# Another order for the first part of a hand-ordered attention-and-maxout kernel

## The chip, the cores and the metric

The kernel runs on one core of one Trainium2 chip. A core has five instruction streams that run side by side: TensorE (PE, matrix products; PEld are its weight loads), VectorE (DVE), ScalarE (ACT), GpSimd (POOL) and SyncE (SP), and 16 DMA engines that SP, ACT and POOL feed through queues of their own. The metric is the device time of one execution in microseconds (us). Three executions of the kernel before gave 153.05 us as their median, 152.96 to 153.08.

## The reference

The input is `x` (8 batches, 8 heads, 512 tokens, 64 wide), `state` (8 batches, 8 heads, 32 states, 64 wide) and four weight matrices. Tokens read the states, states read the tokens, and both results go through a maxout layer with three weights and an output layer:

```python
scores = (x @ state.T) / 8;  a = softmax(scores);   xread = a @ state
scores2 = (state @ x.T) / 8; a2 = softmax(scores2); sread = a2 @ x
y = concat([xread, sread], axis=2)           # 544 rows a batch and head
y = y.transpose(0, 2, 1, 3).reshape(4352, 512)
h = max(y @ w1, y @ w2, y @ w3)              # 512 -> 768
out = h @ w_out                              # 768 -> 512
```

## The kernel before

Products run in bf16 with f32 sums. The token rows are not formed as `xread` first. For each batch the kernel multiplies the states into the weights (`G = state @ w`, one row for each head and state, 3 x 768 columns) and then `a @ G`, so that the maxout layer works on 256 rows (heads times states) in place of 512. The middle dimension 768 is cut in six slices `m` of 128 columns; a slice of the maxout layer of a batch's 512 tokens is three weights by two halves of those rows, six products of 128 x 128 x 512.

Three plans, written out by hand as strings, hold the whole order of the work: `FIRST` (batches 0 and 1, and the preparation of batches 2 and 3), `EACH` (run five times, once a batch, in a steady rhythm) and `LAST`. `perform` (L543) reads a plan and calls one function for each step; each function issues its instructions, DMAs too, on the engine that the step names (`S`, `P`, `A`, `D` for SP, POOL, ACT, DVE). An engine runs its instructions strictly in the order of issue, so the place of a step in the string is its place in the queue of its engine, and nothing else decides the order. Waits between engines follow from the data and from the buffers.

The steps that the change moves, with the numbers being batch and slice, or parity `g` of the heads (even heads are g = 0, odd ones g = 1):

- `lst k` loads the states of batches 2k and 2k+1 (L153); `stc` casts them to bf16 (L216), `stt` transposes them on PE (L221), `stp` copies them into the block-diagonal tile `bd` in two halves (L227).
- `lxu 0 0` loads the even heads of batch 0 as f32 through SP (L174) and `cxu` casts them on DVE (L177). `lxg b g` loads the other halves of x through POOL with a cast on the way (L169). `xt b g` transposes one half on PE (8 instructions, L236), `xtc` copies it to `xT` (L243). `xtd b` (L248) does it for a later batch by a DMA from SP.
- `lw m0 m1 i` loads slices m0 to m1-1 of weight i through POOL (L180), `lwo` the output weight (L185), `lx` a later batch (L164).
- `sc b g` are the scores (8 PE instructions, L261), `ex` the exponentials on ACT (L268), `sum` the row sums and their reciprocals on DVE (L275, L277), `wt` the division (L283), `at b g` turns the weights a on PE (4 instructions, L294), `atc` copies them out (L297); `atd` does it by a DMA (L301).
- `sr b` is the states' reading (32 PE instructions, L326), `srs` its scaling (L339, L342).
- `g b m` is one slice of G (8 PE instructions, L362), `gc` its copy out of PSUM (L380); `gr`, `grc` are the same over wider runs of columns (L362, L402, L405).
- `l1 b m` is one slice of the maxout layer, 6 PE instructions into three banks (L415); `m0` (ACT, L430), `ma` and `mb` (DVE, L435 and L439) take the maximum. `l2 b j` is a quarter of the output layer (6 PE instructions, L446), `l2c` its copy out (L453), `so` the store (L476).
- `busy n` issues n products of zeros on PE that nothing reads (L210). `ident` builds the identity that transposes need (POOL), `pad` makes padded copies of x (POOL, L307 and L310).

PSUM is handed out from the strings `BANKS` (four single banks, one digit for each use) and `PAIRS` (two pairs of banks, for `g`, `gr` and `sc 2`). A step that gets a bank waits until the last reader of that bank has ended; when two engines read one bank's tile in halves (`stp 0 AD`), the second half waits for the first.

Where a step names two engines (`DA`), its two halves go to the two engines in that order.

Of the kernel before, what the change touches and what calls it, by code (L numbers as in the profile page):

```python
# [15 lines left out]


FIRST = """
    lxu 0 0 S; lst 0 A; lxg 1 0; zero; warm; clr 0; clr 1; clr 2; clr 3; stc 0 D; ident; busy 1;
    lst 1 S; busy 2; busy 1; busy 2; busy 1; busy 1; stt 0; busy 1; busy 2; cxu 0 0 D; stp 0 AD;  # L20
    stc 1 A; lxg 0 1; xt 0 0; lxg 1 1; lw 0 1 0; busy 1; lw 0 3 1; xtc 0 0 A; xt 1 0; xones 0; busy 2;
    busy 1; lw 0 2 2; xtc 1 0 DA; sc 0 0; xt 0 1; lw 1 2 0; busy 1; busy 1; lw 2 4 0; lw 2 4 2; sc 1 0;
    ex 0 0; ex 1 0; busy 1; xtc 0 1 A; xt 1 1; busy 1; busy 1; sum 0 0; busy 1; stt 1; lw 3 6 1; busy 1;
    sc 0 1; busy 1; ex 0 1; xtc 1 1 D; busy 1; sc 1 1; ex 1 1; busy 1; stp 1 A; lxg 2 1; wt 0 0 P;
    busy 1; xones 1; at 0 0; sum 1 0; busy 1; busy 1; sum 0 1; sr 0; busy 1; sum 1 1; g 0 0; wt 1 0 P;
    g 1 0; gc 1 0 A; wt 0 1 D; sr 1; busy 1; srs 0; lxg 2 0; at 0 1; at 1 0; wt 1 1 P; atc 0 0 D;
    at 1 1; gc 0 0 D; atc 0 1 A; lw 4 6 2; srs 1; atc 1 0 A; g 1 1; atc 1 1 D; gc 1 1 A; g 0 1;
    l1 0 0 1; g 1 2; m0 0 0; g 0 2; l1 1 0; gc 0 1 D; gc 1 2 A; l1 1 1; m0 1 0; ma 0 0; mb 0 0; ma 1 0;
    lw 4 6 0; mb 1 0; l1 0 1; g 0 3; m0 1 1; g 1 3; gc 0 2 A; l1 0 2; ma 1 1; l1 1 2; xtd 2; pad 2;
    m0 0 1; mb 1 1; ma 0 1; m0 0 2; lst 3 A; gc 0 3 DA; l1 0 3; m0 1 2; lwo; gc 1 3 A; ones; g 0 5;  # L30
    g 1 4; mb 0 1; ma 0 2; lxg 3 0; m0 0 3; mb 0 2; gc 0 5 A; lst 2 S; ma 1 2; l1 1 3; stc 3 P; m0 1 3;
    l1 0 5; mb 1 2; g 0 4; gc 1 4 A; g 1 5; ma 0 3; l1 1 4; m0 0 5; gc 0 4 A; mb 0 3; ma 1 3; m0 1 4;
    lxg 3 1; l1 0 4; sc 2 -; gc 1 5 A; xtd 3; mb 1 3; gr 2 1024 1280; m0 0 4; gr 2 1280 1792; ex 2 -;
    grc 2 1280 1792 A; l1 1 5; m0 1 5; ma 0 5; stc 2 A; mb 0 5; gr 2 512 1024; gr 2 1792 2304; sr 2;
    ma 1 4; mb 1 4; ma 0 4; mb 0 4; l2 0 3; grc 2 512 1024 A; stt 2; grc 2 1024 1280 D; gr 2 0 512;
    l2 0 0; l2 0 1; l2 0 2; grc 2 1792 2304 A; sum 2 -; l2c 0 0 A; grc 2 0 512 A; ma 1 5; wt 2 - P;
    srs 2; l2c 0 3 A; stp 2 A; mb 1 5; l2c 0 2 D; atd 2; so 0 2 4 P; stt 3; l2c 0 1 A; stp 3 DA;
    so 0 0 2 A; lx 4;
"""
EACH = """  # L40
    pad 1; gr 1 1792 2304; gr 1 0 512; grc 1 1792 2304 AD; l2 -1 0; l2 -1 1; l1 0 0; grc 1 0 512 D;
# [22 lines left out]
"""  # L64

BANKS = """
# [3 lines left out]
"""  # L70
PAIRS = """
    0110101010 1010101010 1010101010 1010101010 10
"""


# [601 lines left out]
```

## Time and profile before

| | us |
|---|---|
| median of 3 executions | 153.05 |
| the profiled execution | 152.82 |
| its span, first to last instruction | 151.0 |
| PE busy within the span | 146.6 |
| DVE, ACT, POOL busy | 115.4, 86.2, 54.6 |
| first product of the maxout layer (L415) starts | 16.40 |
| first product of the steady part (`EACH`) starts | 42.72 |

The page sums the span by engine, shows the chain of work that ended last, and groups instructions by source line. A row of the timeline has the start in us from the span's start, the duration, the engine, the line, the operation, the tiles out<-in, the shape and a count; brackets hold the idle time before it and what ended it. A merged row's duration runs to the modelled end of its last instruction, some 0.17 us after PE could issue the next one.

### The profile page before, as it was taken

Reading aid. Unit: us, or ns where it says so; the run is one execution under the profiler, and the core shown is the slowest. Engines: PE = TensorE matmul, PEld = TensorE weight load, DVE = VectorE, ACT = ScalarE, POOL = GpSimd, SP = SyncE. Lnnn points to the kernel's source line nnn. Section 1 sums busy time; section 2 is a strip of 40 time slices with the busy share of each in tenths; the row PEclk is TensorE's granted clock in tenths of the full one; section 3 lists DMA queues with packets and bytes.
Section 4 is the critical chain, followed back from the end, with each engine's and each line's share of the span. In section 5 each row is a group of like instructions: output and inputs, shape, how many; then the busy total and the mean of one; then the engine's idle time right before and its main releaser. Section 6 shows DMA issues by size and latency. Waiting matters only on the chain.

```text
span 151.0 us, 3639 instructions
## 1 busy us (share of the span) xinstructions
PE 146.6 (97%) x1434; PEld 73.6 (49%) x1434; DVE 115.4 (76%) x202; ACT 86.2 (57%) x147; POOL 54.6 (36%) x74
## 2 busy tenths in 40 slices
PE   6999999999999999999999999999999999999992
PEld 2475434344444443444354435443544445679771
DVE  6468899889139899789978997798879887675353
ACT  3567866779695665466646664666466653331220
POOL 6998418302235505550554055404341200001500
PEclk9999999999999999999999999999999999999999
DMA  4999999994658898897599848895503250300545
GB/s 108 245 196 195 198 197 198 143 206 67 125 138 256 109 87 250 103 230 120 173 111 222 154 144 124 213 139 155 205 0 78 80 215 7 133 5 17 190 168 198
DMA packets 38581, 22.30 MB, mean 148 GB/s; under 512 B 22032, under 2 KB 36368, under 8 KB 38560
## 3 DMA queue, kind: packets, MB, share of 16 engines
q0 software_dynamic: 15200, 13.44, 47.3%
q1 hardware_dynamic: 21920, 6.95, 22.8%
q10 hardware_dynamic: 1440, 1.64, 3.6%
q8 instruction: 12, 0.20, 0.5%
q14 instruction: 9, 0.07, 0.2%
HBM read 15.20 MB, written 8.91 MB: 160 GB/s over the span
## 4 chain that ended last, share of the span: by engine, by line
PE 94%; DMA 4%; DVE 1%; issue 1%; POOLq 0%
PE pw L415 47%; PE po L446 25%; PE pg L362 6%; PE po L461 4%; DMA x<-in_x_dram 4%; PE idle L210 3%; PE ps L261 2%; PE psr L326 2%; PE pxt L236 1%; PE pgh L362 1%; PE pat L294 1%; DVE held L521 0%; PE pt L221 0%; PE idle L519 0%; DVE osb L465 0%
## 5 line engine op out<-in xcount | busy, mean ns | idle before, releaser
L415 PE MATMUL pw<-aT,G 128*128 128x512 bf16 x288 | 66.6, 379 | 0.0
L430 ACT CAST t<-pw 128x512 bf16<-128x512 f32 (+1 forms) x54 | 30.4, 562 | 28.7 <-PE pw L415 27.9
L415 PEld LDWEIGHTS <-G 128*128 128x128 bf16 x288 | 27.2, 98 | 33.7 <-issue 2.4
L435 DVE TENSOR_TENSOR t<-t,pw 128x512 bf16<-128x512 bf16 (+1 forms) x54 | 35.3, 653 | 9.9 <-ACT t L430 7.6
L446 PE MATMUL po<-wout,ht 128*128 128x512 bf16 x168 | 39.8, 379 | 0.0
L439 DVE TENSOR_TENSOR ht<-t,pw 128x512 bf16<-128x512 bf16 x48 | 33.0, 687 | 4.6
L283 POOL TENSOR_TENSOR a<-e,rden 128x1024 bf16<-128x1024 bf16 (+1 forms) x9 | 14.9, 1654 | 27.4 <-DVE seen L336 15.1
L446 PEld LDWEIGHTS <-ht 128*128 128x128 bf16 x168 | 15.3, 98 | 19.2 <-issue 2.1
L476 POOL DMA_DIRECT2D out_dram<-osb x12 | 6.9, 578 | 32.6 <-ACT t L430 22.0
L402 ACT CAST G<-pg 128x1024 bf16<-128x1024 f32 (+1 forms) x19 | 16.6, 912 | 0.8 <-PE pg L362 0.8
L453 DVE COPY osb<-po 128x512 f32<-128x512 f32 x14 | 9.6, 687 | 6.8 <-PE po L446 6.8
L310 POOL COPY xp<-x 128x1024 bf16<-128x1024 bf16 x12 | 12.3, 1066 | 5.2 <-DMA x<-in_x_dram 5.2
L453 ACT COPY osb<-po 128x512 f32<-128x512 f32 x15 | 8.9, 594 | 8.8 <-PE po L446 8.8
L275 DVE TENSOR_REDUCE seen<-e 128x32 f32<-128x1024 bf16 (+1 forms) x10 | 10.0, 999 | 2.9 <-ACT e L268 2.9
L268 ACT ACTIVATE e<-ps 128x1024 bf16<-128x1024 f32 (+1 forms) x10 | 8.5, 853 | 5.9 <-PE ps L261 5.8
L210 PE MATMUL idle<-zero 128*128 128x512 bf16 x30 | 10.2, 441 | 1.3 <-DVE zero L188 1.3
L362 PE MATMUL pg<-w,bd 64*32 64x512 bf16 (+1 forms) x288 | 10.8, 362 | 0.0
L402 DVE CAST G<-pg 128x512 bf16<-128x512 f32 (+1 forms) x10 | 9.1, 948 | 1.3 <-ACT G L402 1.3
L471 POOL DMA_DIRECT2D out_dram<-osb x4 | 2.2, 541 | 19.4 <-ACT osb L465 19.4
L380 ACT CAST G<-pg 128x768 bf16<-128x768 f32 (+1 forms) x10 | 7.7, 774 | 2.1 <-PE pg L362 2.1
L415 PE MATMUL pw<-atp,w 128*128 128x256 bf16 x72 | 8.7, 272 | 0.0
L415 PEld LDWEIGHTS <-w 128*128 128x128 bf16 x72 | 6.9, 98 | 1.5
(71 smaller groups left out, 114.1 us busy)
## 6 DMA issues: line engine op xcount, KB each, us to landing
out_dram<-osb POOLq DMA_DIRECT2D x11, 512.0 KB, 3.7
x<-in_x_dram POOLq DMA_DIRECT2D x4, 512.0 KB, 7.5
x<-in_x_dram POOLq DMA_DIRECT2D x7, 256.0 KB, 9.3
w<-in_moe_w_dram POOLq DMA_DIRECT2D x5, 256.0 KB, 8.8
w<-in_moe_w_dram POOLq DMA_DIRECT2D x2, 384.0 KB, 8.7
wout<-in_moe_w_out_dram POOLq DMA_DIRECT2D x1, 768.0 KB, 9.7
out_dram<-osb SPq DMA_DIRECT2D x3, 256.0 KB, 2.3
osb<-in_x_dram SPq DMA_DIRECT2D x1, 512.0 KB, 4.1
```

The source lines that it names most:

```text
L210: nc.tensor.matmul(p, zero[:, 0:128], zero, start=True, stop=True)
L275: nc.vector.reduce_sum(out=den, in_=parity(e[b], g), axis=AX.X)
L283: times[c](out=parity(a[b], g).rearrange("p j g s n -> p j (g s) n"), in0=parity(e[b], g).rearrange("p j g s n -> p j (g s) n"), in1=rdens ...
L310: nc.gpsimd.tensor_copy(out=xp[b][:, :, :, g * (D + 1):g * (D + 1) + D], in_=v[:, g])
L362: nc.tensor.matmul(p(s, g), bd(b, 2 * s + g)[64 * g:64 * g + 64, g, :], f(w_sb[64 * g:64 * g + 64, s]), start=True, stop=True, tile_positi ...
L402: copier[c[g]](out=v[:, g:h], in_=p[:, g:h, 0:c1 - c0])
L415: nc.tensor.matmul(pw[i][:, 0:n], lhs(i, k), rhs(k), start=(k == 0), stop=(k == nk - 1))
L430: nc.scalar.copy(out=t0s[b, m][:, 0:n], in_=open_ps["l", b, m][0][:, 0:n])
L435: nc.vector.tensor_max(t1s[b, m][:, 0:n], t0s.pop((b, m))[:, 0:n], open_ps["l", b, m][1][:, 0:n])
L439: nc.vector.tensor_max(ht[b][:, m, :], t1s.pop((b, m))[:, 0:n], open_ps.pop(("l", b, m))[2][:, 0:n])
L446: nc.tensor.matmul(p, ht[b][:, m, j * 128:(j + 1) * 128], wout_sb[:, m, :], start=(m == 0), stop=(m == NM - 1))
L453: copier[c[i]](out=o[:, j, i * w:i * w + w], in_=p[:, i * w:i * w + w])
```

## The change

Only `FIRST` is rewritten, and with it the strings of banks. The set of steps is the same but for these:

- `lw 2 4 2` (slices 2 and 3 of the third weight, one DMA) becomes `lw 2 3 2` and `lw 3 4 2`; the first now goes ahead of `lw 1 2 0`, the second behind `lxg 2 1`.
- 32 products of zeros stand in the place of 30.
- `ident` is issued behind four loads on POOL, where it was behind one. `lst 1` is on ACT, behind `stc 0`, where it was on SP right behind `lxu 0 0`.
- `stt 1` and its copies come after `sc 1 1`; `stt 2` and `stt 3` stay at the end, with `stp 2` and `stp 3` last.
- `at 1 1` (the odd weights of batch 1) comes after the first `l1`, where it was ahead of it.
- Copies change engines: among others `stc 0` DVE to ACT, `stc 1` ACT to POOL, `wt 0 0` and `wt 2` POOL to DVE, `gc 0 0` DVE to ACT, `gc 0 2` ACT to DVE; `so 0 0 2` ACT to POOL; `stc 2` ACT to DVE, both halves of `stp 3` to DVE; `gc 1 0`, `gc 0 1` and three `grc 2` are shared by ACT and DVE; `lx 4` goes ahead of both stores; `atd 2` goes ahead of `xtd 3`; `ones` is issued earlier.
- The first `l1 0 0` loses its last argument: it takes the two halves of the rows weight by weight, where it took each half for all three weights. In the tail the quarters of `l2 0` come as 3, 2, 0, 1, where they came as 3, 0, 1, 2.

`EACH` and `LAST` are unchanged as text. Their digits in `BANKS` are renamed one for one (3 to 1, 2 to 3, 1 to 2, 0 to 0) and those of `PAIRS` are swapped, so that each step there shares its banks with the same steps as before.

```diff
@@ -16,26 +16,26 @@
 
 
 FIRST = """
-    lxu 0 0 S; lst 0 A; lxg 1 0; zero; warm; clr 0; clr 1; clr 2; clr 3; stc 0 D; ident; busy 1;
-    lst 1 S; busy 2; busy 1; busy 2; busy 1; busy 1; stt 0; busy 1; busy 2; cxu 0 0 D; stp 0 AD;
-    stc 1 A; lxg 0 1; xt 0 0; lxg 1 1; lw 0 1 0; busy 1; lw 0 3 1; xtc 0 0 A; xt 1 0; xones 0; busy 2;
-    busy 1; lw 0 2 2; xtc 1 0 DA; sc 0 0; xt 0 1; lw 1 2 0; busy 1; busy 1; lw 2 4 0; lw 2 4 2; sc 1 0;
-    ex 0 0; ex 1 0; busy 1; xtc 0 1 A; xt 1 1; busy 1; busy 1; sum 0 0; busy 1; stt 1; lw 3 6 1; busy 1;
-    sc 0 1; busy 1; ex 0 1; xtc 1 1 D; busy 1; sc 1 1; ex 1 1; busy 1; stp 1 A; lxg 2 1; wt 0 0 P;
-    busy 1; xones 1; at 0 0; sum 1 0; busy 1; busy 1; sum 0 1; sr 0; busy 1; sum 1 1; g 0 0; wt 1 0 P;
-    g 1 0; gc 1 0 A; wt 0 1 D; sr 1; busy 1; srs 0; lxg 2 0; at 0 1; at 1 0; wt 1 1 P; atc 0 0 D;
-    at 1 1; gc 0 0 D; atc 0 1 A; lw 4 6 2; srs 1; atc 1 0 A; g 1 1; atc 1 1 D; gc 1 1 A; g 0 1;
-    l1 0 0 1; g 1 2; m0 0 0; g 0 2; l1 1 0; gc 0 1 D; gc 1 2 A; l1 1 1; m0 1 0; ma 0 0; mb 0 0; ma 1 0;
-    lw 4 6 0; mb 1 0; l1 0 1; g 0 3; m0 1 1; g 1 3; gc 0 2 A; l1 0 2; ma 1 1; l1 1 2; xtd 2; pad 2;
-    m0 0 1; mb 1 1; ma 0 1; m0 0 2; lst 3 A; gc 0 3 DA; l1 0 3; m0 1 2; lwo; gc 1 3 A; ones; g 0 5;
-    g 1 4; mb 0 1; ma 0 2; lxg 3 0; m0 0 3; mb 0 2; gc 0 5 A; lst 2 S; ma 1 2; l1 1 3; stc 3 P; m0 1 3;
-    l1 0 5; mb 1 2; g 0 4; gc 1 4 A; g 1 5; ma 0 3; l1 1 4; m0 0 5; gc 0 4 A; mb 0 3; ma 1 3; m0 1 4;
-    lxg 3 1; l1 0 4; sc 2 -; gc 1 5 A; xtd 3; mb 1 3; gr 2 1024 1280; m0 0 4; gr 2 1280 1792; ex 2 -;
-    grc 2 1280 1792 A; l1 1 5; m0 1 5; ma 0 5; stc 2 A; mb 0 5; gr 2 512 1024; gr 2 1792 2304; sr 2;
-    ma 1 4; mb 1 4; ma 0 4; mb 0 4; l2 0 3; grc 2 512 1024 A; stt 2; grc 2 1024 1280 D; gr 2 0 512;
-    l2 0 0; l2 0 1; l2 0 2; grc 2 1792 2304 A; sum 2 -; l2c 0 0 A; grc 2 0 512 A; ma 1 5; wt 2 - P;
-    srs 2; l2c 0 3 A; stp 2 A; mb 1 5; l2c 0 2 D; atd 2; so 0 2 4 P; stt 3; l2c 0 1 A; stp 3 DA;
-    so 0 0 2 A; lx 4;
+    lst 0 A; lxu 0 0 S; zero; clr 0; clr 1; clr 2; clr 3; warm; lxg 1 0; lxg 0 1; busy 3; busy 1;
+    lxg 1 1; busy 1; busy 1; lw 0 1 0; stc 0 A; busy 1; cxu 0 0 D; ident; busy 1; busy 1; lst 1 A;
+    busy 1; busy 1; stt 0; ones; xt 0 0; busy 1; busy 1; busy 1; xtc 0 0 D; busy 1; busy 1; lw 0 3 1;
+    stp 0 DA; busy 1; xt 1 0; xt 0 1; xtc 1 0 D; busy 1; busy 1; sc 0 0; xtc 0 1 D; xones 0; xt 1 1;
+    lw 0 2 2; sc 1 0; busy 1; ex 0 0; busy 1; xtc 1 1 A; sum 0 0; busy 1; sc 0 1; busy 1; wt 0 0 D;
+    ex 0 1; sum 0 1; lw 2 3 2; lw 1 2 0; busy 1; busy 2; ex 1 0; busy 1; busy 1; lw 2 4 0; sum 1 0;
+    sc 1 1; lw 3 6 1; stc 1 P; stt 1; busy 1; at 0 0; busy 1; busy 1; xones 1; lxg 2 1; sr 0; ex 1 1;
+    g 0 0; lw 3 4 2; wt 0 1 D; wt 1 0 P; sum 1 1; lxg 2 0; g 1 0; stp 1 A; atc 0 0 A; gc 0 0 A; sr 1;
+    at 1 0; xtd 2; wt 1 1 P; gc 1 0 DA; srs 0; at 0 1; atc 0 1 D; g 0 1; atc 1 0 D; gc 0 1 AD; srs 1;
+    lst 2 S; g 1 1; l1 0 0; m0 0 0; lw 4 6 0; lw 4 6 2; at 1 1; pad 2; gc 1 1 A; ma 0 0; mb 0 0; busy 1;
+    g 1 2; g 0 2; gc 0 2 D; atc 1 1 A; l1 1 0; m0 1 0; l1 1 1; lwo; gc 1 2 A; m0 1 1; l1 0 1; ma 1 0;
+    m0 0 1; g 1 3; mb 1 0; gc 1 3 A; g 0 3; l1 0 2; l1 1 2; ma 1 1; mb 1 1; ma 0 1; m0 0 2; gc 0 3 DA;
+    l1 0 3; lst 3 A; m0 1 2; g 0 5; m0 0 3; gc 0 5 A; g 1 4; l1 1 3; mb 0 1; l1 0 5; ma 0 2; m0 1 3;
+    mb 0 2; lxg 3 0; gc 1 4 A; stc 3 P; ma 1 2; lxg 3 1; ma 0 3; g 0 4; m0 0 5; mb 0 3; g 1 5; gc 0 4 A;
+    l1 1 4; l1 0 4; sc 2 -; mb 1 2; m0 1 4; ma 1 3; gc 1 5 A; mb 1 3; gr 2 1024 1280; gr 2 1280 1792;
+    ma 0 5; m0 0 4; ex 2 -; mb 0 5; l1 1 5; gr 2 1792 2304; ma 1 4; grc 2 1280 1792 A; gr 2 512 1024;
+    m0 1 5; mb 1 4; sr 2; ma 0 4; grc 2 1024 1280 D; mb 0 4; sum 2 -; ma 1 5; wt 2 - D; l2 0 3; srs 2;
+    l2 0 2; l2c 0 3 A; mb 1 5; stc 2 D; grc 2 512 1024 AD; l2 0 0; grc 2 1792 2304 AD; l2c 0 2 A; lx 4;
+    atd 2; stt 2; gr 2 0 512; l2 0 1; grc 2 0 512 DA; stt 3; l2c 0 0 A; xtd 3; stp 3 D; l2c 0 1 D;
+    so 0 0 2 P; so 0 2 4 P; stp 2 A;
 """
...
 BANKS = """
-    0123012301 3023123031 0131310212 1010202320 1203120312 0132103210 2312031201 3201302130 2132021320
-    1302132103 2130231032 1032103210 3102310321 3023102310 2310230213 0231032130 2130213021 3210321302
-    3103210321 0321031023 1032130231 0231032103 2130230230 2310230123 0130230120 3123023123 123013200
+    0123012301 2303032032 1201323230 3023102030 3120210332 0132103120 1321031031 2013201302 1023101320
+    1302103213 2013210312 0132013201 3201203120 1321031203 1203120310 3210312013 2103210321 0321320132
+    1031201320 1320132012 0312013210 3120312013 2013210310 3103120310 2310210310 2301231031 2312310213
+    00
 """
 PAIRS = """
-    0110101010 1010101010 1010101010 1010101010 10
+    0101011010 1010100101 0101010101 0101010101 01
 """
```

## Prediction

> **What bounds the kernel now.** I read the page first, its sum by engine and the chain.
>
> ```profile
> span 151.0 us, 3639 instructions
> ...
> PE 146.6 (97%) x1434; PEld 73.6 (49%) x1434; DVE 115.4 (76%) x202; ACT 86.2 (57%) x147; POOL 54.6 (36%) x74
> ...
> PE 94%; DMA 4%; DVE 1%; issue 1%; POOLq 0%
> ```
>
> PE is busy for 97% of the span and 94% of the chain is PE. Then I read a table by stretches: 16.40 to 33.00 and four rounds of `EACH`, of which the first round and the sum are shown.
>
> ```profile
> 46.04:61.29 15.25, 15.25 (x149) 6.82 (x148) 13.62 (x21) 8.99 (x15) 6.47 (x9) 1.00 0.85 161
> ...
> sum 77.58, PE 77.58 PEld 33.91 DVE 66.98 ACT 48.83 POOL 30.22; mean PE 15.52 PEld 6.78 DVE 13.40 ACT 9.77 POOL 6.04
> ```
>
> The columns are the stretch, its length, PE busy, PEld, DVE, ACT, POOL, the granted clock, DMA. The round is 15.25 us and PE fills it all at clock 1.00, as it fills all five stretches (77.58 of 77.58). `EACH` and `LAST` keep their text, and their banks are only renamed. So the end moves by as much as PE's position at the start of `EACH` moves, unless copies of the first part are still in the way there. The question is then PE's timeline in the head, given here for PE alone.
>
> ```profile
> 1.27 3.43 PE L210 MATMUL idle<-zero 128*128 128x512 bf16 x8 [1.27 <-DVE zero L188]
> 4.54 0.39 PE L221 MATMUL pt<-ident,st 128*128 128x128 bf16 x4
> 4.76 0.81 PE L210 MATMUL idle<-zero 128*128 128x512 bf16 x3
> 5.72 0.62 PE L236 MATMUL pxt<-ident,x 128*128 128x128 bf16 x8
> 6.17 0.38 PE L210 MATMUL idle<-zero 128*128 128x512 bf16 x1
> 6.74 0.62 PE L236 MATMUL pxt<-ident,x 128*128 128x128 bf16 x8 [0.18 <-DMA x<-in_x_dram]
> 7.19 0.81 PE L210 MATMUL idle<-zero 128*128 128x512 bf16 x3
> 7.84 0.40 PE L261 MATMUL ps<-bd,xT 128*128 128x64 bf16 x8
> 8.07 0.61 PE L236 MATMUL pxt<-ident,x 128*128 128x128 bf16 x8
> ...
> 9.44 0.62 PE L236 MATMUL pxt<-ident,x 128*128 128x128 bf16 x8
> ...
> 13.07 0.63 PE L326 MATMUL psr<-x,e 128*32 128x128 bf16 x32
> 13.63 0.39 PE L210 MATMUL idle<-zero 128*128 128x512 bf16 x1
> 13.95 0.52 PE L362 MATMUL pg<-w,bd 64*32 64x384 bf16 x16
> 14.40 0.63 PE L326 MATMUL psr<-x,e 128*32 128x128 bf16 x32
> ...
> 15.19 0.83 PE L294 MATMUL pat<-ident,a 128*128 128x128 bf16 x12
> 15.95 0.52 PE L362 MATMUL pg<-w,bd 64*32 64x384 bf16 x16
> 16.40 1.47 PE L415 MATMUL pw<-aT,G 128*128 128x512 bf16 x6
> 17.80 0.52 PE L362 MATMUL pg<-w,bd 64*32 64x384 bf16 x16
> ```
>
> Prices come from one start to the next: a product of zeros (a filler below) is 0.427 for each of the first eight (4.54 less 1.27, with a faster last one) and (7.84 - 7.19) / 3 = 0.215 later; `xt` 6.17 - 5.72 = 0.45; `sc` 8.07 - 7.84 = 0.23; `stt` and `at` 4.76 - 4.54 = 0.22; `sr` 0.56; two `g` 14.40 - 13.95 = 0.45; an entry into `sr` or `g` costs 0.10 (13.95 - 13.63 - 0.215); `l1` 17.80 - 16.40 - 0.10 = 1.30. PE's waits in the head are what these leave: 5.72 - 4.76 - 0.65 = 0.31 for the cast of x, 6.74 - 6.17 - 0.215 = 0.35 for the x of batch 1, and nothing of note later.
>
> **The change part by part.** *Up to 5.72.* Both orders have eleven fillers and `stt 0` ahead of `xt 0 0`, so PE comes to it at 5.41 either way and waits for the same cast. The loads on POOL, and how long single issues took to land:
>
> ```profile
> 2.81 1.55 POOL L169 DMA_DIRECT2D x<-in_x_dram  x2
> 6.04 3.71 POOL L180 DMA_DIRECT2D w<-in_moe_w_dram  x5
> x<-in_x_dram POOLq DMA_DIRECT2D x1, 256.0 KB, 5.2
> x<-in_x_dram POOLq DMA_DIRECT2D x1, 256.0 KB, 5.8
> w<-in_moe_w_dram POOLq DMA_DIRECT2D x1, 256.0 KB, 7.4
> stf<-in_state_dram SPq DMA_DIRECT2D x1, 128.0 KB, 7.0
> ```
>
> `ident` was over when the two loads behind it began at 2.81. It moves behind three more issues of 1.55 / 2 = 0.78 on POOL, so it is over at 5.15, `stt 0` goes at 5.2 and is done at 5.4. It costs nothing; without the wait for the cast each 0.1 that it is later would cost 0.1.
>
> *The x loads.* The x loads issued at 2.81 and 3.59 land 5.2 and 5.8 later, at 8.01 and 9.4, `lw 0 2 2` (issued at 6.04) at 13.4. In the new order the same bytes lie ahead of each of these on POOL's queue. `lst 1` (128 KB) leaves SP's queue and comes from ACT's at about 4 (an estimate: behind the cast that `stt 0` at 4.54 followed), which is still ahead of or beside those x loads, so I leave their landings where they are.
>
> *5.72 to 13.7, step by step.* `xt 0 0` to 6.17; six fillers to 7.46; `xt 1 0` to 7.91 (its x landed just before 6.74, that wait of 0.35 is gone); `xt 0 1` waits for 8.01, goes at 8.05 (0.14 of wait), to 8.50; two fillers, `sc 0 0` to 9.15; `xt 1 1` waits until 9.44 (0.29, where a filler stood before), to 9.89; `sc 1 0`, three fillers, `sc 0 1`, six fillers to 12.27; `sc 1 1`, `stt 1`, a filler, `at 0 0` to 13.15; two fillers and the entry: `sr 0` at 13.68, against 13.07. The same work is done as before 13.07; three more fillers up to here make 0.65 of the 0.61, and the new waits, 0.43, stand for old ones of 0.35 and 0.03.
>
> *13.7 to the maxout layer.* `sr 0` and an entry to 14.34 (the filler behind each `sr` is gone), two `g` to 14.79, `sr 1` to 15.35, two `at` and an entry to 15.89, two `g` to 16.34: `l1 0 0` at 16.34, against 16.40. Here PE is only a little behind ACT, whose rows are these:
>
> ```profile
> 12.58 1.16 ACT L227 COPY bd<-pt 64x512 bf16<-64x512 bf16 x2
> 14.54 0.80 ACT L380 CAST G<-pg 128x768 bf16<-128x768 f32 x1 [0.80 <-PE pg L362]
> 15.61 1.07 ACT L297 COPY aT<-pat 128x512 bf16<-128x512 bf16 x2 [0.27 <-PE pat L294]
> 17.48 0.59 ACT L430 CAST t<-pw 128x512 bf16<-128x512 f32 x1
> 14.02 1.29 POOL L283 TENSOR_TENSOR a<-e,rden 128x512 bf16<-128x512 bf16 x1 [0.40 <-DVE rden L277]
> ```
>
> `ex 1 1` starts at 12.7 (`sc 1 1` plus 0.2), then two state copies 1.16, `atc 0 0` 0.58, `gc 0 0` 0.80 end at 15.7 or a little later, and the third pair of `g` needs that at 15.89. `wt 1 0` on POOL starts at about 13.8 and takes up to 1.29; `at 1 0` needs it at 15.35. Both fit, by 0.2 and 0.3.
>
> *The turn put behind `l1 0 0`.* `l1 0 0` to 17.64, `at 1 1` 0.22, a filler 0.22, an entry, two `g`: `l1 1 0` at 18.63. Before, it came 0.45 after 17.80, at 18.25. That is +0.37 with the same work done: 0.43 for two fillers over all, 0.14 + 0.29 of new waits for the 0.35 and 0.03 that went, less 0.10 for fewer entries. The cover here is thin: `m0 0 0` starts at 16.97, and with `gc 1 1` (0.80) and `atc 1 1` (0.58) behind it ACT is done between 18.7 and 18.95, as far as starts overlap, while the second product of `l1 1 0` wants it at 18.84. Ends: 0 and 0.3 (when the whole tile must be there at 18.63 and nothing overlaps); I take 0.05.
>
> *The price of a filler.* The row at 1.27 shows eight at 0.427, the row at 4.76 three at half that. The Trainium skill, TensorE: Matmul & The Clock Gate, part 1, says that the halved clock of the start lasts for a span of time of about 3.4 us and not for a number of products. The trace agrees, with 3.3 us from the first product to the first group at the full rate. By that rule the two added fillers run at the full rate and cost 0.43 as above; at the halved clock they would cost 0.85.
>
> *From `l1 1 0` to `EACH`.* The order of `g` and `l1` on PE is the old one up to the tail, and DVE's maxima keep their distance: `gc 0 2`, the copy of a slice (ACT's take 0.80), is new on DVE, but `m0 0 0` is done at 16.97 + 0.59 = 17.56, where it was at 18.07, and `l1 1 0` comes 0.37 later, so that DVE has 0.9 more ahead of `ma 1 0`. Two old waits lie here:
>
> ```profile
> 19.63 2.75 PE L415 MATMUL pw<-aT,G 128*128 128x512 bf16 x12
> 34.04 1.63 PE L415 MATMUL pw<-aT,G 128*128 128x512 bf16 x6
> 34.68 1.01 ACT L402 CAST G<-pg 128x1024 bf16<-128x1024 f32 x1
> ```
>
> `l1 1 1` could go 1.30 after 18.25 and started at 19.63, 0.08 late, for `mb 0 0`; DVE has no room to give that back, so I count half. The group at 34.04 takes 1.63 in place of 1.47: a bank that `mb 0 4` had not read. The new banks give it others, and 0.16 goes; next late is the pair for `gr 2 512 1024`, which comes free with the copy that ends at 34.68 + 1.01 = 35.69 and would be wanted at 34.04 + 1.30 + 0.10 + 0.22 = 35.66. With the way to PE, 0.05, that leaves -0.08.
>
> *The tail.* DVE takes on `wt 2`, `stc 2`, three half copies of G and half of `stp 3`, about 4.4 us, into this gap:
>
> ```profile
> 42.60 0.69 DVE L453 COPY osb<-po 128x512 f32<-128x512 f32 x1 [4.29 <-PE po L446]
> 45.14 1.82 DVE L402 CAST G<-pg 128x512 bf16<-128x512 f32 x2 [1.25 <-ACT G L402]
> 43.27 2.76 PE L446 MATMUL po<-wout,ht 128*128 128x512 bf16 x12
> ```
>
> The gaps of 4.29 and 1.25 hold it. The closest place is the first `l2` of `EACH`: its bank waits for `l2c 0 0` on ACT, behind both halves of the last copy of G. From the end of `gr 2 0 512` that is 0.2 to DVE, 0.69 there, 0.5 from start to start on ACT (1.07 less 0.58, the row at 15.61), 0.58 and 0.05, 2.0 us in all. PE has an `l2` of 1.30, `stt 3` 0.22, an entry 0.10 and two `gr` of 0.45 or more to do, 2.1. It fits by 0.1; I count nothing. `so 0 0 2` from ACT to POOL, `lx 4` issued earlier and `atd 2` ahead of `xtd 3` touch queues on which PE waits first at `l1 2 0`, two `l2` behind the row at 43.27, 2.6 us: 0, with 0.3 as the upper end.
>
> *Sum.* +0.37 + 0.05 - 0.04 - 0.08 = +0.30 us, rounded down to +0.25 since the switch costs are the least sure. The profiled execution would go from 152.82 (span 151.0 and 1.8 around it) to 153.1; the median of the runs stands 0.23 above it, so 153.05 becomes 153.3. A measurement of this kernel can tell about 0.2%, 0.31 us, from no change, and the forecast lies inside that, on the slow side.
>
> **The rivals.** *The walk holds* (0.46): 153.3, itself between 153.1 and 153.5.
>
> *The tail is late, slower* (0.25). DVE has some nine pieces between `sum 2` and the last copy of G. If they follow each other by their full length of 0.69 and not by some 0.60, DVE is 0.8 late, the pair for `gr 2 0 512` comes free after PE asks for it, and the first `l2` of `EACH` waits. It decides from 0.1 us of lateness on; each further 0.1 costs 0.1. Price 0.3 to 0.6: about 153.7. For it speaks that DVE is the engine with the least room (13.62 of 15.25 in the round quoted), against it that its wait of 4.29 ended only with PE.
>
> *The x lands earlier, not slower* (0.18). The last row of the loads shows a state load of 128 KB beside running loads of POOL: 7.0 us to land. If `lst 1` on ACT's queue is pushed aside like that, its 128 KB of f32 are out of the x loads' way, 0.35 us, as a quarter of the 512 KB that such a load reads in the 1.4 between 8.01 and 9.4, both new waits shrink by up to 0.29, and the time is 153.0. The Trainium skill, DMA: Bandwidth & Descriptors, Queues, rings and completion order, says that a DMA engine alternates between its queues packet by packet. By that rule `lst 1` would be through within a microsecond, the x loads land as before and the time is 153.3. The 7.0 speaks against an even alternation there; which of the two holds at 4 us no row shows.
>
> *POOL is held* (0.05). `stc 1` now waits on POOL for `lst 1`, and `lxg 2 1`, `lw 3 4 2`, `wt 1 0` are queued behind it, 2.4 us of work ahead of 14.0. It decides when `lst 1` lands after 11.6, that is, 7.6 us after its issue; a microsecond beyond costs PE one at `at 1 0`: 154.3.
>
> *Otherwise* (0.06). Faster than 152.8 it cannot be by this stream: with every wait of the head gone but the cast's, it is 0.43 - 0.38 - 0.10 - 0.15 = -0.2.
>
> **How the numbers follow.** Forecast 153.3. Of the walk's 0.46, 0.32 lie within 0.2% and 0.14 above; of the tail's 0.25, 0.22 above; of the early x's 0.18, 0.15 within and 0.03 below; POOL 0.05 above; the rest in thirds. Faster 0.05, same 0.52, slower 0.43. The range takes the early x and the tail's full price: 152.9 to 153.8.
>
> **What would show it.** In PE's timeline: `xt 0 0` at 5.7 again, `xt 1 0` at 7.5 with no wait, short waits before 8.05 and 9.44; `sr 0` at 13.7, `l1 0 0` at 16.3 to 16.5, `l1 1 0` at 18.6 to 18.8, the first `l2` of `EACH` at 43.5 (43.27 before); rounds of 15.25 again. Wrong it would be by x landing well before 8.0 and 9.4, by a wait of PE for ACT or DVE ahead of the third pair of `g` or of `l1 1 0`, or by waits between 40 and 47.

## The result, and the profile after

The changed kernel took 154.21 us (median, 153.58 to 154.44) where the kernel before, measured beside it, took 153.06 (152.96 to 153.61): a ratio of 1.0061, 95% interval 1.0034 to 1.0087. By the ratio that is slower by 0.9 us (0.5 to 1.3; the two medians are 1.15 apart), where 0.25 had been forecast, and 154.21 lies above the range, which ended at 153.8. The profiled execution took 154.17 with a span of 152.4, so its trace stands for the median.

The page of the changed kernel, its sum by engine and the chain that ended last; then, from the chain in order of time, its one long piece that is not PE, and below it the one of the kernel before:

```profile
span 152.4 us, 3642 instructions
...
PE 147.3 (97%) x1436; PEld 74.2 (49%) x1436; DVE 120.7 (79%) x210; ACT 82.7 (54%) x144; POOL 53.5 (35%) x75
...
PE 91%; DMA 5%; POOL 1%; issue 1%; DVE 1%; POOLq 0%
```
```profile
3.02 7.32 DMA x<-in_x_dram
```
```profile
1.37 5.32 DMA x<-in_x_dram
```

PE is as busy as before. But its share of the chain fell from 94% to 91%: the x load that the chain goes through now lands at 10.34, where the one before landed at 6.69. The stretches from the first `l2` of `EACH` on (columns as in the prediction's table) say that the steady part is as before:

```profile
44.55:59.85 15.30, 15.30 (x156) 6.86 (x149) 13.64 (x22) 9.94 (x18) 5.49 (x7) 1.00 0.63 130
59.85:75.10 15.25, 15.25 (x156) 6.81 (x149) 12.89 (x20) 9.06 (x16) 6.02 (x8) 1.00 0.80 158
```

So the loss lies ahead of 44.55, against 43.27 before: 1.28 us in these two executions. PE's timeline of the changed kernel shows where (every line number is one higher than before; in most kernels of the experiments below it is two higher):

```profile
1.28 4.54 PE L211 MATMUL idle<-zero 128*128 128x512 bf16 x11 [1.28 <-DVE zero L189]
5.65 0.39 PE L222 MATMUL pt<-ident,st 128*128 128x128 bf16 x4
5.87 0.61 PE L237 MATMUL pxt<-ident,x 128*128 128x128 bf16 x8
6.32 1.46 PE L211 MATMUL idle<-zero 128*128 128x512 bf16 x6
7.62 0.61 PE L237 MATMUL pxt<-ident,x 128*128 128x128 bf16 x8
8.74 0.62 PE L237 MATMUL pxt<-ident,x 128*128 128x128 bf16 x8 [0.51 <-DMA x<-in_x_dram]
...
10.39 0.62 PE L237 MATMUL pxt<-ident,x 128*128 128x128 bf16 x8 [0.36 <-DMA x<-in_x_dram]
...
16.80 0.64 PE L363 MATMUL pg<-w,bd 64*32 64x384 bf16 x16
17.38 1.47 PE L416 MATMUL pw<-aT,G 128*128 128x512 bf16 x6
...
19.22 0.52 PE L363 MATMUL pg<-w,bd 64*32 64x384 bf16 x16
19.67 0.61 PE L416 MATMUL pw<-aT,G 128*128 128x512 bf16 x2
```

`xt 1 1` starts at 10.39 (9.44 before): 0.95 later. `l1 1 0` starts at 19.67 (18.25 before): 1.42 later. From the one to the other are 9.28, against 8.81. I call this the stretch below. The 1.42 is then 0.95 of x and 0.47 of stretch, and 0.14 of it is won back before 44.55.

The issues of the second and third x load and of `lst 1`, each with its time to land, and the DMA queues between 7 and 8 us (packets, MB, and the share of the 16 engines; q0 is POOL's queue, q10 ACT's), first of the changed kernel, then of the kernel before:

```profile
x<-in_x_dram POOLq DMA_DIRECT2D x1, 256.0 KB, 6.4
...
x<-in_x_dram POOLq DMA_DIRECT2D x1, 256.0 KB, 7.3
stf<-in_state_dram ACTq DMA_DIRECT2D x1, 128.0 KB, 6.2
...
q0 software_dynamic: 319, 0.16, 118.4%
q10 hardware_dynamic: 46, 0.05, 17.0%
```
```profile
q0 software_dynamic: 394, 0.19, 145.0%
```

The x loads were issued at 2.27 and 3.02, earlier than before, and landed at 8.69 and 10.35, later than the 8.01 and 9.40 of before. `lst 1`, issued on ACT at 3.67, has no packet until 7.3 and lands at 9.9, so it moves just when PE waits for x.

### The profile page after: what moved, and what is told of

Its sections match the earlier page's. It is cut to its first block, busy times and chain, and to the rows that moved or that the text cites. A ratio compares the mean times of both kernels' runs of the same rounds, so it can differ in the third digit from the quotient of the medians.

```text
span 152.4 us, 3642 instructions
## 1 busy us (share of the span) xinstructions
PE 147.3 (97%) x1436; PEld 74.2 (49%) x1436; DVE 120.7 (79%) x210; ACT 82.7 (54%) x144; POOL 53.5 (35%) x75
## 4 chain that ended last, share of the span: by engine, by line
PE 91%; DMA 5%; POOL 1%; issue 1%; DVE 1%; POOLq 0%
PE pw L416 47%; PE po L447 25%; PE pg L363 6%; DMA x<-in_x_dram 5%; PE po L462 4%; PE ps L262 2%; PE psr L327 2%; PE idle L211 2%; PE pgh L363 1%; POOL x L170 1%; PE pat L295 1%; DVE held L522 0%; PE pt L222 0%; PE pxt L237 0%; PE idle L520 0%
## 5 line engine op out<-in xcount | busy, mean ns | idle before, releaser
L477 POOL DMA_DIRECT2D out_dram<-osb x13 | 7.4, 569 | 43.9 <-ACT t L431 27.7
L284 POOL TENSOR_TENSOR a<-e,rden 128x1024 bf16<-128x1024 bf16 (+1 forms) x7 | 11.9, 1697 | 20.3 <-DVE seen L337 10.3
L403 ACT CAST G<-pg 128x1024 bf16<-128x1024 f32 (+1 forms) x19 | 15.3, 840 | 3.0 <-DVE G L403 1.9
L403 DVE CAST G<-pg 128x512 bf16<-128x512 f32 (+1 forms) x13 | 11.1, 888 | 0.1
L472 POOL DMA_DIRECT2D out_dram<-osb x4 | 2.2, 541 | 19.4 <-ACT osb L466 19.4
L181 POOL DMA_DIRECT2D w<-in_moe_w_dram x10 | 7.7, 788 | 0.0
```

Source lines behind the costliest of these rows:

```text
L284: times[c](out=parity(a[b], g).rearrange("p j g s n -> p j (g s) n"), in0=parity(e[b], g).rearrange("p j g s n -> p j (g s) n"), in1=rdens ...
L403: copier[c[g]](out=v[:, g:h], in_=p[:, g:h, 0:c1 - c0])
```

## The experiments

Three theories stood at first. **S**: the state load on ACT's queue moves among the x loads and makes them late. **P**: the x loads are late because POOL issues three in a row and `ident` behind them. **C**: the other 0.47 is the stretch, that is, fillers, scores and copies between `xt 1 1` and `l1 1 0`. In the table the x column is the landing of the last x load that `xt 1 1` needs; x, `xt 1 1`, `l1 1 0` and the stretch are of one profiled execution of each, and landings differ by some tenths from one execution to the next. The time is the median, the ratio is to the kernel before, measured beside it.

| kernel | x | `xt 1 1` | `l1 1 0` | stretch | time | ratio, 95% interval |
|---|---|---|---|---|---|---|
| before | 9.40 | 9.44 | 18.25 | 8.81 | 153.06 | |
| after | 10.35 | 10.39 | 19.67 | 9.28 | 154.21 | 1.0061, 1.0034 to 1.0087 |
| after, states on SP | 9.68 | 9.72 | 19.00 | 9.28 | 153.66 | 1.0042, 1.0024 to 1.0061 |
| before, states on ACT | 10.00 | 10.04 | 18.85 | 8.81 | 153.45 | 1.0032, 1.0013 to 1.0050 |
| after, `ident` early | 10.01 | 10.05 | 19.33 | 9.28 | 153.87 | 1.0047, 1.0031 to 1.0062 |
| after, two fillers less | 10.06 | 10.11 | 19.35 | 9.24 | 154.09 | 1.0066, 1.0044 to 1.0087 |
| after, states on POOL | 10.55 | 10.59 | 19.87 | 9.28 | 153.94 | 1.0051, 1.0034 to 1.0068 |
| the same, `ident` early | 9.66 | 9.71 | 18.99 | 9.28 | 153.71 | 1.0031, 1.0015 to 1.0047 |
| before, states on POOL | 9.41 | 9.53 | 18.92 | 9.39 | 153.55 | 1.0037, 1.0024 to 1.0050 |
| before, states behind W | 9.63 | 9.92 | 18.96 | 9.04 | 153.72 | 1.0029, 1.0015 to 1.0043 |
| before, other states early | 10.32 | 10.37 | 19.18 | 8.81 | 153.36 | 1.0008, 0.9998 to 1.0018 |
| before, other states midway | 10.21 | 10.27 | 19.09 | 8.82 | 153.48 | 1.0012, 0.9994 to 1.0031 |
| before, two fillers more | 9.73 | 9.78 | 19.02 | 9.24 | 153.64 | 1.0033, 1.0021 to 1.0045 |
| states on SP, scores early | 9.43 | 9.69 | 19.18 | 9.49 | 153.82 | 1.0046, 1.0031 to 1.0061 |
| the same, two fillers less | 9.65 | 9.71 | 19.08 | 9.37 | 153.87 | 1.0053, 1.0033 to 1.0073 |
| the same, `wt 0 1` on POOL | 9.57 | 9.61 | 18.65 | 9.04 | 153.40 | 1.0016, 1.0000 to 1.0032 |

**The states on SP again, in the new order.**

```diff
-    lst 0 A; lxu 0 0 S; zero; ... busy 1; lst 1 A;
+    lst 0 A; lxu 0 0 S; lst 1 S; zero; ... busy 1;
```

> The changed kernel with one step put back: lst 1 on SP right behind lxu 0 0, as before the change. Theory S (the state load on ACT's queue runs through the x loads): the x loads that PE waits for land at about 8.0 and 9.4 again instead of 8.7 and 10.35, PE starts xt 1 1 near 9.45 instead of 10.39, and the time falls by 0.6 to 1.0 us, to about 0.2 to 0.4 us over the kernel before. Theory P (the loads are late because they are issued on POOL without ident between them, during DVE's clearing): the x loads still land at 8.6 or later and 10.2 or later, and the time stays about 1 us over the kernel before.

The last x load landed 0.67 earlier than in the changed kernel, not quite at the 9.4 that S had promised, and the median fell by 0.55, a little less than its 0.6 to 1.0; the two intervals overlap. The stretch stayed at 9.28.

**The states on ACT, in the old order.**

```diff
-    stc 0 D; ident; busy 1; lst 1 S; ... stp 0 AD; stc 1 A; ... stt 1; lw 3 6 1;
+    stc 0 A; lst 1 A; ident; busy 1; ... stp 0 AD; ... stc 1 P; stt 1; lw 3 6 1;
```

> The kernel before with the state load alone moved: stc 0 on ACT, lst 1 on ACT behind it, and stc 1 on POOL ahead of lw 3 6 1 (so that ACT does not stand still for it). Theory S: lst 1 lands near 9.9, the second and third x loads land at about 8.7 and 10.3 instead of 8.0 and 9.4, and the kernel is 0.5 to 1.0 us slower than before. Theory P: the x loads land at 8.0 and 9.4 within 0.2, and the time is within 0.3 us of before.

The same step made the old order slower, and PE's timeline of that kernel shows x as the cause and nothing else:

```profile
8.70 0.62 PE L238 MATMUL pxt<-ident,x 128*128 128x128 bf16 x8 [0.20 <-DMA x<-in_x_dram]
10.04 0.62 PE L238 MATMUL pxt<-ident,x 128*128 128x128 bf16 x8
...
18.85 1.47 PE L417 MATMUL pw<-aT,G 128*128 128x512 bf16 x6
```

`xt 1 1` is 0.60 later than in before and `l1 1 0` is 0.60 later: the old stretch of 8.81, only moved. The median is 0.36 above the 153.09 measured beside it (0.49 by the ratio), where S had said 0.5 to 1.0.

**`ident` early, in the new order.**

```diff
-    lxg 1 0; lxg 0 1; ... cxu 0 0 D; ident; busy 1;
+    lxg 1 0; ident; lxg 0 1; ... cxu 0 0 D; busy 1;
```

> The changed kernel with ident put back behind the first x load on POOL. Theory S: nothing but ident moves, the x loads still land near 8.7 and 10.35, the time is within 0.3 us of the changed kernel (about 1 us over the kernel before). Theory P: the x loads land at 8.0 and 9.4, the time falls by 0.6 to 1.0 us.

The last x load landed at 10.01, still 0.6 late, and the time did not return. P does not explain the changed kernel.

**Two fillers less, in the new order.**

```diff
-    lw 1 2 0; busy 1; busy 2; ex 1 0; busy 1; busy 1; lw 2 4 0;
+    lw 1 2 0; busy 2; ex 1 0; busy 1; lw 2 4 0;
```

> The changed kernel with two of the six products of zeros between sc 0 1 and sc 1 1 left out. By the prediction's sum a filler is 0.215 us on PE's path: 0.43 us less. Rival: the division of batch 1's weights (POOL at 14.76 to 16.05, wanted by at 1 0 at 16.25) and the copies on ACT (gc 0 0 ends at 16.66, wanted at 16.80) take over after 0.1 to 0.2: no more than 0.2 us less.

Two products of 0.215 were taken out and the stretch fell by 0.04, from 9.28 to 9.24. The time did not move. The time came back as waits: 0.2 before one of the remaining fillers, whose cause the trace does not tell plainly, and the rest in small pieces from `at 1 0` on. `at 1 0` waits for POOL, which divides until 15.76, after waiting for DVE's reciprocals, and `g 1 1` behind it waits for ACT's half of `gc 1 0`:

```profile
14.47 1.29 POOL L285 TENSOR_TENSOR a<-e,rden 128x512 bf16<-128x512 bf16 x1 [2.45 <-DVE rden L279]
```

So C in the form "the fillers are what makes it long" falls for the new order. Whether a filler costs anything in the old order was still open.

**Two fillers more, in the old order.**

```diff
-    sc 0 1; busy 1; ex 0 1;
+    sc 0 1; busy 3; ex 0 1;
```

> The kernel before with two more fillers (0.43 of TensorE) between batch 0's odd scores and batch 1's. Theory C in the prediction's form (TensorE's own walk sets this stretch in before, so a filler is paid in full): the stretch from the last turn of x (9.44) to layer 1 of batch 1 goes from 8.81 to about 9.24 and the time to 153.4 to 153.5. Rival (the copies on ACT and DVE set it in before too, and the fillers fall into waits that stand behind them): a stretch of 9.0 or less and a time of 153.0 to 153.2.

PE's timeline of this kernel, `xt 1 1` and `l1 1 0`:

```profile
9.78 0.62 PE L238 MATMUL pxt<-ident,x 128*128 128x128 bf16 x8 [0.23 <-DMA x<-in_x_dram]
...
19.02 1.25 PE L417 MATMUL pw<-aT,G 128*128 128x512 bf16 x5
```

19.02 - 9.78 = 9.24, which is 8.81 and 0.43: in the old order PE sets the stretch and two fillers are paid in full, as the prediction priced them; the median, 153.64, is 0.52 above the 153.12 beside it. In the new order other engines have come up to the same length, so that taking the fillers away uncovers them. The next three kernels say which. All have the states on SP.

**Scores early.** Batch 1's even scores go back ahead of `xt 1 1`, into PE's wait for x, with their exponential and sum.

```diff
-    xones 0; xt 1 1; lw 0 2 2; sc 1 0; busy 1; ex 0 0; ... wt 0 0 D; ... busy 2; ex 1 0; ... sum 1 0; sc 1 1;
+    xones 0; sc 1 0; xt 1 1; lw 0 2 2; busy 1; ex 0 0; ex 1 0; ... wt 0 0 D; sum 1 0; ... busy 2; ... sc 1 1;
```

> The changed kernel with the states back on SP (153.66 in its run) and batch 1's even scores back ahead of the last turn of x, their exponential right behind batch 0's, their sum two places earlier on DVE. Theory C (the stretch from the last turn of x to layer 1 is 0.47 longer because the scores of 0.23 and one more filler of 0.22 now stand in it): the scores fill the wait of 0.29 for the last x load, the stretch falls from 9.28 to about 9.05, and the time is 153.4 to 153.5. Rival (the stretch is set by the copies and the division of batch 1's weights, not by what TensorE has in it): it stays at 9.2 or more, the time at 153.6 to 153.7.

The stretch grew to 9.49. Its timeline names what came late:

```profile
11.70 1.24 PE L212 MATMUL idle<-zero 128*128 128x512 bf16 x4 [0.30 <-ACT xT L245]
```

`xtc 1 1` on ACT now stands behind a second exponential, and a filler waited for the bank that it empties. PE's 0.23 fewer were no gain, since PE was not what set the length.

**The same with two fillers less.** Those at `busy 1` (bank 0) and the last of the six go.

```diff
-    busy 1; busy 2; busy 1; busy 1; lw 2 4 0; sc 1 1;
+    busy 2; busy 1; lw 2 4 0; sc 1 1;
```

> The kernel of the run with the early scores, and two of the six fillers between the odd scores of batch 0 and those of batch 1 left out (0.43 of TensorE's time). Theory C with the division as what held the run with two fillers less: batch 1's even weights are now divided more than a microsecond earlier, so the 0.43 is gained nearly whole, the stretch falls to about 8.65 and the time to 153.0 to 153.1. Rival (the copies on ACT between the odd scores and the second product that builds G hold it, or the copy of the last turned x): half of it or less, a stretch of 8.85 or more and a time of 153.25 or more, with waits where the fillers stood or before those products.

9.37, the rival's figure. PE's fourth product pair `g 1 1` (the second half of the group) waits, and DVE's timeline shows why; first PE, then DVE:

```profile
15.67 0.36 PE L364 MATMUL pg<-w,bd 64*32 64x384 bf16 x8
16.50 0.36 PE L364 MATMUL pg<-w,bd 64*32 64x384 bf16 x8 [0.48 <-ACT G L382]
```
```profile
11.93 0.68 DVE L277 TENSOR_REDUCE seen<-e 128x16 f32<-128x512 bf16 x1
12.64 0.25 DVE L279 RECIPROCAL rden<-seen 128x16 f32<-128x16 f32 x1
12.81 0.63 DVE L277 TENSOR_REDUCE seen<-e 128x16 f32<-128x512 bf16 x1
...
13.76 0.88 DVE L285 TENSOR_TENSOR a<-e,rden 128x512 bf16<-128x512 bf16 x1
14.57 0.67 DVE L277 TENSOR_REDUCE seen<-e 128x16 f32<-128x512 bf16 x1
15.28 0.25 DVE L279 RECIPROCAL rden<-seen 128x16 f32<-128x16 f32 x1
15.45 0.50 DVE L382 CAST G<-pg 128x384 bf16<-128x384 f32 x1
```

The wait is put down to ACT's half of `gc 1 0`, but that half follows DVE's, which begins only at 15.45. DVE had no pause from 11.93 on: sum, sum, division, sum, then the copy.

**The same with one division on POOL.**

```diff
-    lw 3 4 2; wt 0 1 D; wt 1 0 P; sum 1 1;
+    lw 3 4 2; wt 1 0 P; wt 0 1 P; sum 1 1;
```

> The kernel with the early scores and two fillers less (153.87), and the division of batch 0's odd weights moved from DVE to POOL, where it fits behind that of batch 1's even ones. Theory C, now with DVE as what holds the stretch (sum, sum, division, sum, then the half copy that frees the banks of the fourth product that builds G, which waited 0.48 at 16.50): that wait goes to 0.1 or less, the stretch from the last turn of x to layer 1 of batch 1 falls from 9.37 to about 8.9, and the time to 153.4. Rival (ACT holds it, DVE is only the last to be named): the wait stays at 0.3 or more, the stretch at 9.2 or more, the time at 153.7 to 153.9.

The wait of 0.48 is gone, DVE now waits for PE, and the time is the forecast 153.40 (0.47 less; the intervals do not overlap, if barely). DVE, then PE:

```profile
14.61 0.56 DVE L382 CAST G<-pg 128x384 bf16<-128x384 f32 x1 [0.27 <-PE pg L364]
```
```profile
15.58 0.64 PE L364 MATMUL pg<-w,bd 64*32 64x384 bf16 x16
...
17.99 0.73 PE L364 MATMUL pg<-w,bd 64*32 64x384 bf16 x16
18.65 1.68 PE L417 MATMUL pw<-aT,G 128*128 128x512 bf16 x7
```

9.04 in place of the forecast 8.9: the group at 17.99 takes 0.73 where 0.52 is usual, so 0.2 of wait stands there that I had not seen. Against the kernel with the states on SP alone, 153.66 and 9.28, these steps together are worth 0.24 of stretch and 0.26 of time, and those two intervals overlap. C holds in this form: in the new order PE's walk and DVE's chain to `gc 1 0` are about equally long, so that shortening PE's part alone paid 0.04 or nothing. A shorter DVE chain with all of PE's work left in place was not run; as the prediction's walk without waits is 9.19, it could give 0.09 at most, by estimate.

**Which part of S.** In the changed kernel POOL's stream also starts earlier, at 4.16 in place of 4.54, as SP's queue is shorter. Rival **B**: it is this start, beside the end of SP's x load, that slows the stream, not the states. Four kernels take the states out of the way by POOL's own queue:

```diff
 after:            -  lst 1 A;                 +  lxg 1 1; lst 1 P;
 after, ident:     -  cxu 0 0 D; ident;        +  lxg 1 0; ident;      (and the line above)
 before:           -  lst 1 S; ... stc 1 A;    +  lxg 1 1; lst 1 P; ... stc 1 P; stt 1;
 before, behind W: -  lst 1 S; ... stc 1 A; ... stt 1;   +  lw 0 1 0; lst 1 P; ... xtc 0 1 A; stc 1 A; ... ex 1 1; stt 1;
```

> The changed kernel with the second load of states taken from ACT's queue and put on POOL's, behind the last of the three x loads, where it cannot run beside or ahead of any of them. Theory S (the load of the states runs in the middle of the x loads and costs them 0.6 to 0.95 us): the last x load lands at 9.0 to 9.2 us, earlier than the 9.40 of before, since SP's queue no longer carries those 131 KB either; the last turn of x starts at about 9.2 (the walk, no longer the load, sets it), the first product of layer 1 for batch 1 comes 9.28 later, at 18.5, and the time is 153.1 to 153.3. Rival (the x loads are late because POOL's queue itself runs slower in this order, whatever else is moved): the last x load lands at 9.7 or later and the time is 153.7 or more.

> The run with the states on POOL's queue (153.94, last x load at 10.55) with the identity matrix made behind the first x load, as in before. Theory P (three x loads issued in a row, the identity only behind W's first slice, slow POOL's stream): the last x load lands at 9.5 or earlier, as in before with the states on POOL (9.41), and the time is 153.3 to 153.5. Rival B (the stream that starts at 4.15 beside SP's load is slowed whatever stands between the issues): it lands at 9.9 or later again, the time is 153.7 to 154.0.

> The kernel before with the second load of states on POOL's queue behind the last x load and its cast on POOL ahead of the second turn of states. Theory S: the x loads land about 0.35 earlier than in before (POOL's first packets come at about 4.2 instead of 4.54 and meet no other load), the two waits for x of 0.14 and 0.29 on TensorE go, the first product of layer 1 for batch 1 moves from 18.25 to about 17.9, and the time is 152.7 to 152.9, faster than before. Rival (W's first slices, 0.35 later behind the states, or the cast on POOL, take the gain back): 153.0 to 153.3, with a wait for W before the first product that builds G.

> The kernel before with the second load of states on POOL's queue behind the first slice of W, its cast on ACT behind the copy of batch 0's odd turned x, its turn on TensorE behind batch 1's odd scores. Theory S: nothing else moves while the x loads do; they land at about 6.4, 7.7 and 9.0, the two waits for x of 0.14 and 0.29 go, and the time is 152.75 to 152.95. Rival B (a stream of POOL that starts beside the end of SP's x load, at 4.2 instead of 4.5, is slowed and gains nothing): the last x load lands at 9.3 or later and the time is 153.0 to 153.4.

None gave what S had promised; the first, with 10.55 and 153.94, came out as its rival had it. All four streams started at 4.03 to 4.20, and the last x load landed at 9.41, 9.63, 9.66 and 10.55, with 9.40 in before: the earlier start, by 0.34 or more, bought nothing. In part these kernels made waits of their own. With `stc 1` on POOL, behind a landing at 9.74, the division that follows is late (stretch 9.39), and with the cast on ACT and `stt 1` behind `sc 1 1` the old order's stretch grew to 9.04, so their times don't measure x alone. For the 10.55 P would be an answer, though it did not explain the changed kernel, as `ident` is the only difference to the 9.66. But the 10.55 comes from the slowest of that kernel's five executions, 154.56, and the medians, 153.94 and 153.71, have overlapping intervals. What made it late stays open.

Two more kernels leave `lst 1` on SP, so that POOL starts late, and move another load of 128 KB, `lst 3`, from 23.41 to the front of ACT's queue:

```diff
 early:   -  l1 0 3; m0 1 2; lst 3 A; ...     +  clr 3; lst 3 A; stc 0 D;
 midway:  -  stc 0 D; ... lst 3 A; ...        +  clr 3; stc 0 A; lst 3 A;
```

> The kernel before with one line moved: the load of the fourth pair of states, 131 KB from ACT's queue, is issued behind the warm-up of ACT at about 3 us instead of at 23.41. The second pair stays on SP, so POOL's stream starts at 4.5 as in before. Theory S (a state load from ACT's queue that moves while the x loads do takes its bytes and some rate from them): the last x load lands at 9.8 to 10.1 instead of 9.40, and the time is 153.4 to 153.6. Rival B (what makes the x loads late is that POOL's stream starts at 4.15, beside the end of SP's x load): it starts at 4.5 here, the last x load lands at 9.3 to 9.6, and the time is 153.0 to 153.2.

> As the run before it (which issued the extra load at 1.36, so that it was through by 6 us and ahead of most of the x loads), but with the first state cast on ACT and the load of the fourth pair of states behind it, as the changed kernel has the second pair: issued at about 3.5, it moves between 6 and 9. The second pair stays on SP, so POOL's stream starts at 4.5. Theory S (it is the place in the middle of the x loads that costs): the last x load lands at 9.8 to 10.1, the time is 153.4 to 153.6. Rival B (the early start of POOL's stream is what costs): it lands at 9.3 to 9.6, the time is 153.1 to 153.3.

The first issued its load at 1.36, before the x loads moved, and so tells nothing of S and B: POOL's stream started at 4.89 and x was late with it in the profiled execution, which at 153.88 was the slowest of that kernel; its median, 153.36, is not distinguishable from before. The second is the test. The load was issued at 3.67, as in the changed kernel, and POOL's stream started at 4.46. POOL's and ACT's queues between 7 and 8 us, and `xt 1 1`:

```profile
q0 software_dynamic: 254, 0.12, 91.4%
q10 hardware_dynamic: 139, 0.13, 40.9%
```
```profile
10.27 0.61 PE L237 MATMUL pxt<-ident,x 128*128 128x128 bf16 x8
```

POOL's queue moved 0.12 MB in that microsecond where it moved 0.19 in before, and the last x load landed 0.81 later. B is not needed for the delay; the states alone do it.

How large is it? Single executions differ too much to read it from two of them. In the six kernels of the table with the second pair of states on SP and nothing added early on ACT, the last x load landed at 9.40 to 9.73; in the five with a state load from ACT's queue amid the x loads it landed at 10.00 to 10.35. The two groups do not overlap, and their middles, 9.61 and 10.06, are 0.45 apart. The 9.40 of before and the 10.35 of after, from which the 0.95 was read, are the two ends. In the median the step is worth +0.24 us here (the interval reaches from -0.06% to +0.31%, so the time alone does not show it), 0.36 with the states on ACT in the old order (0.49 by the ratio) and 0.55 in the new one (0.3 by the ratios).

No kernel tried beats the kernel before. The best, with the states on SP, the scores early, two fillers less and one division on POOL, takes back 0.8 of the 1.15 us between the medians.

## Why the prediction was wrong

**The step that failed: "The x loads".** It said that `lst 1` "is still ahead of or beside those x loads, so I leave their landings where they are". Beside them is not where they are: between 7 and 8 us `lst 1` moved 0.05 MB and POOL's queue gave way from 0.19 to 0.16 (between 7 and 9: 0.12 MB, and from 0.38 to 0.29), and the loads landed 0.68 and 0.95 later. The term was put at nothing; in the two traces it is 0.95 of the 1.04 by which `l1 1 0` missed its forecast of 18.63, and over the kernels of the table about 0.45. The other half of the 0.95 belongs to these two executions; its cause is open. The row of 7.0 us for a state load stood in the prediction, and it was read as a load pushed out of the way; it was a load that would come late and then take its share.

**The walk** was right. From `xt 1 1` to `l1 1 0` it made 18.63 - 9.44 = 9.19; the trace has 9.28. So 0.38 of the 0.47 by which the stretch grew was in the forecast. The 0.09 lies at the third pair of `g`, 0.64 long at 16.80 where 0.52 is usual. The two fits that were checked held: `gc 0 0` ended at 16.66 for the 16.80, and POOL's division at 16.05 for `at 1 0` at 16.25. What had not been timed is `gc 1 0`: DVE's half came first, ACT's ended at 17.04, and `g 1 1`, the second half of the pair, went at 17.09 where it could have gone at 17.03. `l1 0 0` then lost about as much again, waiting for DVE's copy of turned weights. DVE's half of `gc 1 0`, then ACT's `gc 0 0` and its half of `gc 1 0`:

```profile
15.94 0.50 DVE L381 CAST G<-pg 128x384 bf16<-128x384 f32 x1
15.85 1.19 ACT L381 CAST G<-pg 128x768 bf16<-128x768 f32 x2
```

The price of "0.43 for two fillers over all" was confirmed to the hundredth in the old order; that in the new order they cover a DVE chain of the same length was not seen.

**Up to 5.72**: `xt 0 0` went at 5.87, behind `stt 0` at 5.65 in place of 5.2. From the first filler to `stt 0` were 4.37, not 3.27 + 0.65, since ten of the eleven fillers went at about the slow price and not eight. It mattered little: the cast of x ended only at 5.79, and the waits for x behind it swallowed the rest.

**The turn behind `l1 0 0`**: taken at 0.05, it cost nothing; the two `g` at 19.22 end in time and `l1 1 0` follows at 0.45.

**The two old waits** were counted at -0.04 and -0.08. The shift fell from 1.42 at `l1 1 0` to 1.28 at the first `l2` of `EACH`, so -0.14: 0.07 and 0.16 of them went, and waits of about 0.07 are new in between.

**The tail** was right at nothing: from the first `l2 0` to the first `l2` of `EACH` are 44.55 - 37.81 = 6.74, before 43.27 - 36.54 = 6.73. That rival falls.

**The rivals.** "The x lands earlier" named the right load with the wrong sign. "POOL is held" did not happen: `stc 1` ran at 9.95, right when the states landed, and POOL then stood idle for 2.63 until DVE's reciprocals. A rival in which `lst 1` delays x was missing, and so the range ended too low: 153.3 and 0.45 are 153.75, just within it, and with the 0.95 of the profiled execution 154.25. That this is near the 154.21 is in part luck, as the executions of the changed kernel went from 153.58 to 154.44.

The page quoted there, the Trainium skill, DMA: Bandwidth & Descriptors, Queues, rings and completion order, has the DMA engines alternate between queues. The run with the other states midway agrees once the load moves, 0.13 MB against 0.12 in the same microsecond; in the changed kernel both queues moved too, but less evenly, 0.05 against 0.16. My reading of it, that the load would be through within a microsecond of its issue and x would land as before, did not follow: in both kernels it began more than 3 us after its issue, and what it then moved POOL's queue moved less.

## What to carry to other kernels

A transfer moved to another queue is not free because that queue is empty: ask in which microseconds its bytes will move, and whose bytes move then; a load that nobody waits for should be through before the loads that are waited for, as on SP here, where x landed at 9.40 to 9.73. (Behind them x landed at 9.41 to 9.66 in three kernels of four, but none of these was faster than the kernel before.) Where a part has fillers, taking them out, or adding some, shows whether the engine itself or a chain hidden under them sets the length; here two fillers less gave 0.04 of the stretch, and earlier scores, fewer fillers and a division moved off DVE gave 0.24 together.

## What the hardware showed that was not expected

- A load issued on ACT's queue at 3.67, with that queue empty, had no packet until 7.3 (6.9 with the other states midway, and 6.1 to 7.0 in three kernels that issued it at 3.47 to 3.56) while SP's queue ran until about 5 and POOL's from about 4.2 on, and it took 6.2 us to land (4.9 to 5.7 in the others); the same 128 KB issued at 1.37 on SP took 3.9. Why it waits so long no run shows.
- POOL's stream started 0.34 to 0.51 earlier in the kernels whose SP queue was shorter, and the last x load landed earlier in none of them. In the changed kernel and in the one with the states on POOL, single packets of 512 B took up to 1.1 and 1.6 us between 4 and 6.2, where the median packet takes 0.06. The cause is open.
- The first products of zeros take 0.427 us each and later ones 0.215. How long the slow price lasts differed between executions of the same order of PE: the first eleven took 4.04 to 4.87 us.
